# A list scheduler with other times for DMA landings and ScalarE handovers, and another table of ranks: the same instructions of an attention and two feed-forward layers in another order

## The chip, the cores and the metric

The kernel runs on one core of a Trainium2 chip. The time is the device time of one execution in microseconds. Of the kernel before, three runs gave 799.81, 796.45 and 795.07 us; their median is 796.45 us. The smallest change that a measurement of this kernel tells from none is about 0.5%, some 4 us.

## The reference: what is computed

Everything is float32. An attention of 2 batches x 8 heads, 768 positions of 64 elements, in which a query sees the keys of its own hash bucket alone, feeds two feed-forward layers over 1536 tokens:

```python
mask = q_bucket[:, :, :, None] == k_bucket[:, :, None, :]     # 6 sign bits of q @ proj, k @ proj
scores = np.where(mask, scale * np.matmul(q, k.transpose(0, 1, 3, 2)), -1000000000.0)
attn = np.exp(scores - np.max(scores, axis=-1, keepdims=True))
x = np.matmul(attn / (np.sum(attn, -1, keepdims=True) + 1e-09), v)      # -> 1536 x 512
h = np.maximum(x @ w_in, 0.0)                  # 512 -> 2048
x = (s * (h * h) + b) @ w_out                  # 2048 -> 512
out = (((x @ w1) * (x @ w2)) @ w3) @ w_out2    # 512 -> 1024 -> 1024 -> 512
```

## The kernel before, in words

**Numbers and products.** Each float32 operand is held as a high and a low part (fp32r), and each product is three matmuls. TensorE (PE) has the bulk: 4464 matmuls.

**Attention.** 16 heads of three units each, 48 units of 256 queries, numbered m = 0 to 47. A unit has two scores (`score0`, `score1`, tile `sc`, two PSUM buffers in all). For each: VectorE (DVE) takes the row maximum (`negm`, L499), a gate (L507) and a bias (L514); ScalarE (ACT) the exponential (`p`, L522). PE then turns p in three pairs (tile `t`, L536); each pair is split into high and low (`pt`) by ACT and DVE (L574, L578), the middle pair by ACT and GpSimd (POOL) (L557, L562, L568); PE multiplies by v (tile `o`, L542 and L543). ACT shifts half of `o` into `tmp` (L591), and DVE adds (`xf`, L595). The normalising factors are turned on PE too (tile `rt`, L632). The row masks `mm` come from `bits` (PE L463, DVE L468).

**First layer.** In batch 0's half (`h0`, `o0`) the weights arrive as raw float64 pieces of 512 KB (`raw_wi`, `raw_wo`), are converted in six steps (three on DVE, L322, L323 and L329; the others on ACT or POOL) into `w_wi`, `w_wo`, and are written back to memory (`kept_wi`, `kept_wo`). Batch 1's half (`h1`, `o1`) loads them again, 32 loads, into a pool of eight places (`wpool`), so a load waits on its queue until PE has read what stood in the place. PE makes `h`, then `x`, both at L717.

**Second layer.** When the last attention rows are done, the attention's tiles are closed and the second layer's opened (`reopen`). w3 and w_out2 are folded into one matrix on PE (tile `psw`, L929): 8 pieces of w_out2 and 16 of w3 are loaded raw and converted through two raw buffers (`raw2`). Then PE makes `a`, `b` (L717) and `y` (L968).

**What sets the order.** Every operation is recorded with its engine, an assumed time and a rank; a list scheduler (`Plan.emit`) then plays the program through on a clock of its own and issues on each engine, whenever it is free in that clock, the operation of the lowest cost: its rank, plus `LOSS` times the wait until it could start. Ranks come from due times, traced back from the end with the factors `SLACK` and the table `AT`, plus the table `SHIFT`. `TAIL` is what passes from an operation's end to its result, `LAG_TO` what the next engine needs, `PORT` names operations of DVE that can't run beside POOL's. Each engine's instructions then run on the chip in just the order that came out; DMAs are all issued by SyncE (SP), in one queue, in order.

Of the kernel before, what the change touches and what calls it, by code (L numbers as in the profile page):

```python
# [28 lines left out]
U = 256  # L29
# [5 lines left out]
LAG = 1  # L35
# [5 lines left out]
SLACK = dict(dma=0.3103, pe=0.4501, dve=0.4044, act=0.4169, pool=0.3583)  # L41
AT = {
# [10 lines left out]
}  # L53
HOLD = {"conv0_wi_0_0": 85.69, "conv0_wo_0_0": 118.54}
LATER = 1e9
SHIFT = {
# [24 lines left out]
    "kh_los/pool": 12.61, "kh_up0": -55.2, "kh_up1": -59.35, "kh_ups": -29.69, "kh_ups/dve": -53.6,  # L81
    "kh_ups/pool": 22.16, "lo00": 6.66, "lo01": -3.17, "lo0s": -50.9, "lo20": -30.38, "lo21": -5.15, "lo2s":
    -53.13, "load_b": 16.32, "load_p": -65.51, "load_qk0": -18.65, "load_qk1": 17.96, "load_qks": -36.78,
# [3 lines left out]
    "mks/dve": 16.57, "mks/pool": -23.64, "mq0": 33.96, "mq1": -43.58, "mqs": -30.74, "mqs/dve": 17.21,  # L87
# [5 lines left out]
    48.83, "qhs/pool": 83.58, "ql0": -40.32, "ql1": 8.23, "qls": 10.71, "qls/dve": -21.69, "qls/pool": -67.67,  # L93
# [15 lines left out]
}  # L109


def r32(ap):
    return ap.bitcast(F32)


class Slot:
# [17 lines left out]
class Plan:  # L134
# [42 lines left out]
    def locks(self, o, e):  # L177
        return e == "pool" or e == "dve" and o["key"].startswith(self.PORT)
# [4 lines left out]
    def emit(self):  # L183
        for o in reversed(self.ops):
            e, us, _ = o["ways"][0]
# [38 lines left out]
        t = 0.0  # L224
# [60 lines left out]
def lsh_attention_moe(ctx: ExitStack, tc: tile.TileContext, qT, kT, vl, projp, w_in, w_out, sv, bv, w12, w3T, wo2, out):  # L285
    nc = tc.nc
# [743 lines left out]
```

## Time and profile before

| | |
|---|---|
| median of three runs | 796.45 us |
| the profiled execution | 796.26 us, of which the span of its instructions is 794.5 us |
| PE busy | 760.0 us (96%) |
| DVE, ACT, POOL busy | 511.5, 393.6, 337.5 us |
| PE clock granted | full, but for the first microseconds |
| DMA | 110.83 MB in 36172 packets, mean 140 GB/s |

PE is busy through the whole span; the other engines are busy in its first two thirds, while attention, weight conversions and the first layer run, and nearly idle from 620 us on, where only `a`, `b` and `y` are left. The idle microseconds of PE and what ended them stand in the trace's waits; the same view for DVE shows where the engine that feeds it waited.

### The profile page before, as it was taken

To read this page: it belongs to the slowest core of one execution; us is meant where nothing else is said; L and a number is where in the kernel's file an instruction comes from. 1 tells how busy PE (TensorE), PEld (TensorE's weight loads), DVE (VectorE), ACT (ScalarE), POOL (GpSimd) and SP (SyncE) were. 2 spreads that over 40 slices of the span, in tenths; PEclk is the share of its full clock that TensorE was granted. 3 is DMA by queue.
4 is the path that set the end of the run, shared out by engine and by line. 5 is a ranking of instruction groups with operands and counts; after the bars stand their busy time and mean duration, and the time that the engine had idled before them with its cause. 6 is when DMAs were issued, how large, how long until landed. Compare 5 with 4: busy or idle time off the path is not lost.

```text
span 794.5 us, 12256 instructions
## 1 busy us (share of the span) xinstructions
PE 760.0 (96%) x4464; PEld 708.8 (89%) x4464; DVE 511.5 (64%) x1008; ACT 393.6 (50%) x754; POOL 337.5 (42%) x373
## 2 busy tenths in 40 slices
PE   5899999899999999999998999999999999999998
PEld 4788888789898998999998988989999999999996
DVE  4898898899899888899867666675687101010110
ACT  5788887886657546658543433433535111211112
POOL 3477668764755655545322232331327121121212
PEclk9999999999999999999999999999999999999999
DMA  8454344674657646573649886656231000000001
GB/s 211 108 134 119 91 104 116 204 210 134 196 175 233 176 160 184 174 219 108 212 159 324 280 293 242 223 178 207 83 105 54 1 1 14 26 14 21 7 14 66
DMA packets 36172, 110.83 MB, mean 140 GB/s; under 512 B 5136, under 2 KB 7312, under 8 KB 36112
## 3 DMA queue, kind: packets, MB, share of 16 engines
q1 hardware_dynamic: 36112, 110.06, 44.5%
q8 instruction: 35, 0.57, 0.3%
q14 instruction: 25, 0.20, 0.1%
HBM read 68.22 MB, written 24.12 MB: 116 GB/s over the span
## 4 chain that ended last, share of the span: by engine, by line
PE 62%; DVE 13%; ACT 9%; DMA 8%; issue 4%; POOL 4%; SPq 0%; ACTq 0%; POOLq 0%; DVEq 0%
PE h L717 10%; PE x L717 9%; PE a L717 8%; PE b L717 8%; PE y L968 8%; PE sc L489 4%; PE psw L929 4%; PE t L536 4%; ACT p L522 3%; DVE negm L499 3%; DMA raw_w<-in_w3T 3%; PE o L543 2%; PE o L542 2%; DVE pt L578 2%; ACT pt L574 1%
## 5 line engine op out<-in xcount | busy, mean ns | idle before, releaser
L717 PE MATMUL h<-x,w_wi 128*128 128x384 f32 x768 | 152.9, 341 | 2.3 <-DVE rl L793 0.9
L717 PE MATMUL x<-g,w_wo 128*128 128x384 f32 x768 | 151.5, 340 | 3.7 <-DMA w_wo<-kept_wo 1.4
L717 PEld LDWEIGHTS h<-x,w_wi 128*128 128x128 f32 x768 | 132.2, 188 | 8.4 <-DVE rl L793 3.3
L717 PEld LDWEIGHTS x<-g,w_wo 128*128 128x128 f32 x768 | 132.3, 188 | 8.2 <-issue 2.3
L522 ACT ACTIVATE p<-sc,bias,gate 128x768 f32<-128x768 f32 x96 | 95.6, 996 | 26.8 <-DVE bias L514 23.8
L953 DVE SCALAR_TENSOR_TENSOR ab<-b,ab 128x384 f32<-128x384 f32 x32 | 17.8, 557 | 132.4 <-ACT ab L950 102.4
L499 DVE TENSOR_REDUCE negm<-sc 128x1 f32<-128x768 f32 x96 | 90.9, 951 | 10.1 <-PE sc L489 9.6
L489 PE MATMUL sc<-k,q 128*128 128x384 f32 x384 | 89.9, 357 | 6.7 <-ACT p L522 5.2
L536 PE MATMUL t<-ident,p 128*128 128x128 f32 x576 | 85.8, 277 | 6.9 <-ACT p L522 4.3
L959 POOL TENSOR_TENSOR abt<-ab,abt 128x384 fp32r<-128x384 f32 x32 | 33.6, 1051 | 137.9 <-ACT abt L956 137.9
L536 PEld LDWEIGHTS t<-ident,p 128*128 128x128 f32 x576 | 68.0, 142 | 16.4 <-ACT p L522 7.4
L717 PE MATMUL a<-x,w_w 128*128 128x384 f32 x384 | 79.7, 335 | 0.0
L717 PE MATMUL b<-x,w_w 128*128 128x384 f32 x384 | 79.6, 335 | 0.0
L489 PEld LDWEIGHTS sc<-k,q 128*128 128x128 f32 x384 | 65.2, 193 | 11.6 <-ACT p L522 8.7
L542 PE MATMUL o<-pt,vv 128*128 128x256 f32 x288 | 74.1, 290 | 0.5 <-DVE gate L507 0.5
L543 PE MATMUL o<-pt,vv 128*128 128x256 f32 x288 | 72.3, 284 | 2.2 <-POOL pt L568 1.2
L578 DVE TENSOR_TENSOR pt<-t,pt 128x512 fp32r<-128x512 f32 x96 | 65.6, 685 | 9.8 <-ACT pt L574 9.0
L332 POOL TENSOR_TENSOR w_w<-raw_w,w_w 128x512 fp32r<-128x512 f32 x30 | 40.6, 1356 | 67.1 <-ACT w_w L330 66.6
L717 PEld LDWEIGHTS a<-x,w_w 128*128 128x128 f32 x384 | 67.8, 188 | 1.2 <-ACT ab L950 0.2
L956 ACT CAST abt<-ab 128x384 fp32r<-128x384 f32 x32 | 16.5, 516 | 104.7 <-PE y L968 96.7
L717 PEld LDWEIGHTS b<-x,w_w 128*128 128x128 f32 x384 | 67.9, 188 | 0.0
L968 PE MATMUL y<-whl,abt 128*128 128x512 f32 x288 | 67.5, 390 | 0.0
(99 smaller groups left out, 1283.3 us busy)
## 6 DMA issues: line engine op xcount, KB each, us to landing
kept_wo<-w_wo SPq DMA_DIRECT2D x24, 512.0 KB, 5.9
w_wo<-kept_wo SPq DMA_DIRECT2D x24, 512.0 KB, 5.2
raw_wi<-in_w_in SPq DMA_DIRECT2D x16, 512.0 KB, 4.5
raw_wo<-in_w_out SPq DMA_DIRECT2D x16, 512.0 KB, 4.6
kept_wi<-w_wi SPq DMA_DIRECT2D x16, 512.0 KB, 5.4
raw_w<-in_w SPq DMA_DIRECT2D x16, 512.0 KB, 4.4
w_wi<-kept_wi SPq DMA_DIRECT2D x16, 512.0 KB, 5.7
raw_w<-in_w3T SPq DMA_DIRECT2D x16, 512.0 KB, 4.4
```

What stands on the lines that cost most here:

```text
L332: lambda: nc.gpsimd.tensor_tensor(hl()[:, 1], w, r32(hl()[:, 0]), ALU.subtract),
L489: nc.tensor.matmul(sc()[:, i, :HALF], x[:, t], y[:, i * HALF : (i + 1) * HALF], start=st, stop=not st)
L499: lambda j=j, sc=sc: nc.vector.tensor_reduce(negm()[:, j : j + 1], sc()[:, :, :HALF], AX.XY, ALU.max, negate=True),
L522: lambda j=j, k=k, sc=sc: nc.scalar.activation(ps[j](), sc()[:, :, :HALF], AF.Exp, bias=bias()[:, j : j + 1], scale=gate()[:, j : j + 1], ...
L536: nc.tensor.transpose(tp()[:, e, j * P : (j + 1) * P], flat[:, c * P : (c + 1) * P], ident)
L542: nc.tensor.matmul(o()[:, :U], w, pt()[:, 0, e], start=(c == 0), stop=False)
L543: nc.tensor.matmul(o()[:, :U], w, pt()[:, 1, e], start=False, stop=(c == NC - 1))
L578: lambda tp=tp, pt=pt: nc.vector.tensor_tensor(pt()[:, 1], tp(), r32(pt()[:, 0]), ALU.subtract),
L717: nc.tensor.matmul(ps()[:, :n], x, y, start=(i == 0 and e == 0), stop=(i == len(terms) - 1 and e == 2))
L929: nc.tensor.matmul(ps(), w3()[:, p, c], wo()[:, q], start=(j == 0 and e == 0), stop=(j == 7 and e == 2))
L959: lambda: nc.gpsimd.tensor_tensor(abt()[:, 1], ab()[:, :TG], r32(abt()[:, 0]), ALU.subtract),
L968: nc.tensor.matmul(y(), abt()[:, p, c], wt()[:, q], start=(i == 0 and e == 0), stop=(i == DF2 // P - 1 and e == 2))
```

## The change

No instruction's work is changed. The scheduler's constants are: a DMA's result is given a further delay by its kind (`LATE`), handing over to ScalarE costs 0.085 in place of 0.037, several DVE and POOL operations are assumed to take longer (the bias 0.13 in place of 0.07), weight loads 1.3 in place of 1.46 (plus the new delay), and the tables `SLACK`, `AT`, `HOLD`, `SHIFT`, `AHEAD` and `LOSS` have other numbers throughout. Operations that may run on either of two engines can change sides: POOL has 15 instructions fewer and ACT 17 more.

```diff
-SLACK = dict(dma=0.3103, pe=0.4501, dve=0.4044, act=0.4169, pool=0.3583)
+SLACK = dict(dma=0.3391, pe=0.5535, dve=0.5716, act=0.4427, pool=0.4279)
 AT = {
-    "Wh": -4.86, "Wl": -0.88, "a": 53.23, "ab": 73.2, "abh": 79.81, "abl": 23.45, "add0": -0.46, "add1": -2.1,
+    "Wh": 6.26, "Wl": -2.82, "a": 32.88, "ab": 54.41, "abh": 54.36, "abl": 27.77, "add0": -2.95, "add1": 0.02,
...
-HOLD = {"conv0_wi_0_0": 85.69, "conv0_wo_0_0": 118.54}
+HOLD = {"conv0_wi_0_0": 67.61, "conv0_wo_0_0": 28.59}
...
-    LAG_TO = dict(dma=0.1, pe=0.055, dve=0.035, act=0.037, pool=0.085)
-    AHEAD, LOSS = dict(dma=0.079, pe=0.191, dve=0.043, act=0.334, pool=0.249), 21.169
+    LAG_TO = dict(dma=0.1, pe=0.055, dve=0.04, act=0.085, pool=0.095)
+    AHEAD, LOSS = dict(dma=1.714, pe=0.058, dve=0.072, act=0.268, pool=0.156), 39.709
...
+    LATE = dict(raw_=1.1, save_=1.5, again_w12=0.6, again_=0.3, load_=0.6, kh_=0.3, qh=0.3)
...
+    def late(self, o):
+        return next((v for k, v in self.LATE.items() if o["engine"] == "dma" and o["key"].startswith(k)), 0.0)
...
-                end = free[e] + self.TAIL[e]
+                end = free[e] + self.TAIL[e] + self.late(o)
...
-                    f"bias{j}{ph}", "dve", 0.07, LATER,
+                    f"bias{j}{ph}", "dve", 0.13, LATER,
...
-                f"shift{ph}", "act", 0.27, m + LAG + 0.9, lambda: nc.scalar.copy(tmp()[a], o()[z, :U]), [(o, 2)], [(tmp, 0)]
+                f"shift{ph}", "act", 0.39, m + LAG + 0.9, lambda: nc.scalar.copy(tmp()[a], o()[z, :U]), [(o, 2)], [(tmp, 0)]
...
-                f"raw_{key}", "dma", 1.46, LATER,
+                f"raw_{key}", "dma", 1.3, LATER,
...
-                f"square{b}", "dve", 0.47, rank + 0.01,
+                f"square{b}", "dve", 0.53, rank + 0.01,
```

**Place 1: DVE at the program's start.** In names, the first number after `sc_`, `negm_` or `gate_` is the unit, the last a running number; `sw` is a scale made of the scalar input `s_bc`, which a DMA brings. DVE before, from the second half of unit 0's mask on:

```order
L468 TENSOR_SCALAR mm_1_232<-bits_1_1_212,thr_72,sgn_73 128x384
L499 TENSOR_REDUCE negm_0_241<-sc_0_0_227 128x1
L499 TENSOR_REDUCE negm_0_241<-sc_0_1_236 128x1
L507 TENSOR_SCALAR gate_0_248<-negm_0_241 128x1 x2
L514 TENSOR_SCALAR bias_0_251<-negm_0_241,gate_0_248 128x1 x2
L499 TENSOR_REDUCE negm_1_274<-sc_1_0_261 128x1
L371 TENSOR_SCALAR sw_70<-s_bc_68 128x1
L507 TENSOR_SCALAR gate_1_291<-negm_1_274 128x1
L514 TENSOR_SCALAR bias_1_293<-negm_1_274,gate_1_291 128x1
L578 TENSOR_TENSOR pt_0_2_283<-t_0_2_276,pt_0_2_283 128x512
```

DVE now, in two pieces; from the scale on:

```order
L375 TENSOR_SCALAR sw_70<-s_bc_68 128x1
L428 CAST k1_0_185<-q1_0_181 64x768
L472 TENSOR_SCALAR mm_0_209<-bits_0_0_197,thr_72,sgn_73 128x384
L472 TENSOR_SCALAR mm_0_209<-bits_0_1_205,thr_72,sgn_73 128x384
L428 CAST k2_0_187<-mm_0_209 64x768
L472 TENSOR_SCALAR mm_1_230<-bits_1_1_218,thr_72,sgn_73 128x384
```

and from the first maximum of unit 0 on:

```order
L503 TENSOR_REDUCE negm_0_238<-sc_0_0_225 128x1
L503 TENSOR_REDUCE negm_0_238<-sc_0_1_232 128x1
L511 TENSOR_SCALAR gate_0_250<-negm_0_238 128x1
L472 TENSOR_SCALAR mm_1_230<-bits_1_0_242,thr_72,sgn_73 128x384
L518 TENSOR_SCALAR bias_0_253<-negm_0_238,gate_0_250 128x1
L511 TENSOR_SCALAR gate_0_250<-negm_0_238 128x1
L518 TENSOR_SCALAR bias_0_253<-negm_0_238,gate_0_250 128x1
L503 TENSOR_REDUCE negm_1_279<-sc_1_0_265 128x1
L511 TENSOR_SCALAR gate_1_288<-negm_1_279 128x1
L518 TENSOR_SCALAR bias_1_296<-negm_1_279,gate_1_288 128x1
```

The scale stood between the maximum and the gate of unit 1; now it stands ahead of the first masks, and its DMA is sixth on SP's queue, ahead of the weights, where it was the 18th. One half of head 1's mask (`mm_1`) now stands before unit 0's first bias.

**Place 2: ACT and DVE where unit 5 ends and unit 8 begins.** `p_8_0` is the exponential of unit 8's first score, `tmp_5` unit 5's shift, `xf_2` the sum that adds it. ACT before:

```order
L574 CAST pt_6_0_779<-t_6_0_743 128x512
L557 COPY pf_7_1_792<-t_7_1_781 128x512
L407 CAST q1_4_798<-t_4_423 128x768
L522 ACTIVATE p_8_0_821,ssum_2_666<-sc_8_0_756,bias_8_813,gate_8_795 128x768
L591 COPY tmp_5_838<-o_5_772 64x256
L522 ACTIVATE p_8_1_842,ssum_2_666<-sc_8_1_786,bias_8_813,gate_8_795 128x768
L574 CAST pt_6_2_855<-t_6_2_808 128x512
```

ACT now:

```order
L578 CAST pt_5_2_775<-t_5_2_743 128x512
L526 ACTIVATE p_7_1_780,ssum_2_670<-sc_7_1_730,bias_7_739,gate_7_737 128x768
L561 COPY pf_7_1_799<-t_7_1_792 128x512
L595 COPY tmp_5_815<-o_5_759 64x256
L526 ACTIVATE p_8_0_817,ssum_2_670<-sc_8_0_770,bias_8_813,gate_8_811 128x768
L411 CAST q1_4_834<-t_4_392 128x768
L578 CAST pt_7_0_849<-t_7_0_827 128x512
```

DVE before, round the sum that reads `tmp_5`:

```order
L514 TENSOR_SCALAR bias_8_813<-negm_8_777,gate_8_795 128x1
L499 TENSOR_REDUCE negm_8_777<-sc_8_1_786 128x1
L507 TENSOR_SCALAR gate_8_795<-negm_8_777 128x1
L514 TENSOR_SCALAR bias_8_813<-negm_8_777,gate_8_795 128x1
L595 TENSOR_TENSOR xf_2_551<-o_5_772,tmp_5_838 64x256
L636 TENSOR_TENSOR xf_2_551<-rt_5_818,xf_2_551 128x256
L499 TENSOR_REDUCE negm_9_864<-sc_9_0_844 128x1
```

DVE now:

```order
L503 TENSOR_REDUCE negm_8_797<-sc_8_0_770 128x1
L511 TENSOR_SCALAR gate_8_811<-negm_8_797 128x1
L518 TENSOR_SCALAR bias_8_813<-negm_8_797,gate_8_811 128x1
L599 TENSOR_TENSOR xf_2_566<-o_5_759,tmp_5_815 64x256
L503 TENSOR_REDUCE negm_8_797<-sc_8_1_806 128x1
L511 TENSOR_SCALAR gate_8_811<-negm_8_797 128x1
L518 TENSOR_SCALAR bias_8_813<-negm_8_797,gate_8_811 128x1
L503 TENSOR_REDUCE negm_9_856<-sc_9_0_842 128x1
```

The shift stood behind the exponential of `sc_8_0` and the sum behind both of unit 8's biases; now the shift stands ahead of that exponential, and the sum between the two maxima.

**Place 3: SP's queue where the second layer opens.** `raw_wo2` are the raw pieces of w_out2 (in the trace `raw_wo<-in_wo`; those of w3 are `raw_w<-in_w3T` there), `w_wo_1_0_0` to `w_wo_1_0_3` the four loads for batch 1's first `x` products. Before:

```order
L675 DMA raw_wo2_0_0_0_5504<-in_wo2 128x1024
L675 DMA raw_wo2_0_0_1_5523<-in_wo2 128x1024
L705 DMA w_wo_1_0_0_5552<-kept_wo_0_0_0_130 128x1024
L705 DMA w_wo_1_0_1_5569<-kept_wo_0_0_1_131 128x1024
L705 DMA w_wo_1_0_2_5582<-kept_wo_0_0_2_132 128x1024
L705 DMA w_wi_1_1_0_5602<-kept_wi_0_1_0_134 128x1024
L675 DMA raw_wo2_0_1_0_5647<-in_wo2 128x1024
L675 DMA raw_wo2_0_1_1_5664<-in_wo2 128x1024
L695 DMA kept_wo2_0_0_0_158<-w_wo2_0_0_0_5620 128x1024
L705 DMA w_wo_1_0_3_5698<-kept_wo_0_0_3_133 128x1024
```

Now:

```order
L709 DMA w_wo_1_0_0_5433<-kept_wo_0_0_0_130 128x1024
L709 DMA w_wo_1_0_1_5446<-kept_wo_0_0_1_131 128x1024
L709 DMA w_wo_1_0_2_5461<-kept_wo_0_0_2_132 128x1024
L709 DMA w_wo_1_0_3_5483<-kept_wo_0_0_3_133 128x1024
L679 DMA raw_wo2_0_0_0_5546<-in_wo2 128x1024
L679 DMA raw_wo2_0_0_1_5579<-in_wo2 128x1024
L679 DMA raw_wo2_0_1_0_5673<-in_wo2 128x1024
L709 DMA w_wi_1_1_0_5703<-kept_wi_0_1_0_134 128x1024
```

The fourth load stood behind four raw pieces, a load for batch 1's next weights and a store; now the four stand together ahead of every raw piece. Further on, all eight `raw_wo2` now stand ahead of the first `raw_w3`, where they alternated.

## Rows read from the trace of the kernel before

**Rows 1.** The page: busy us (share of the span) and instructions.
```profile
PE 760.0 (96%) x4464; PEld 708.8 (89%) x4464; DVE 511.5 (64%) x1008; ACT 393.6 (50%) x754; POOL 337.5 (42%) x373
```
**Rows 2.** Busy time by stretch: length, then busy us (instructions) of each engine.
```profile
0.00:20.00 20.00, 10.56 (x34) 8.57 (x35) 8.25 (x28) 10.01 (x15) 6.45 (x11) 0.92 0.82 210
20.00:180.00 160.00, 147.65 (x1026) 134.87 (x1025) 142.72 (x326) 131.55 (x262) 110.06 (x137) 1.00 0.52 137
180.00:420.00 240.00, 234.57 (x1474) 223.43 (x1473) 207.92 (x412) 145.61 (x283) 125.04 (x138) 1.00 0.56 177
420.00:600.00 180.00, 176.28 (x931) 163.46 (x930) 122.42 (x199) 67.16 (x118) 55.61 (x50) 1.00 0.61 211
600.00:794.00 194.00, 190.91 (x1007) 178.49 (x1005) 30.17 (x48) 39.32 (x79) 40.34 (x37) 1.00 0.06 22
```
**Rows 3.** Who waited for whom, 20 to 180 us: us in total, times, longest.
```profile
PE t L536 <- ACT p L522: 4.3, 8, 1.0
PE sc L489 <- ACT p L522: 2.7, 5, 0.8
...
DVE pt L578 <- ACT pt L574: 5.0, 13, 0.9
DVE xf L595 <- ACT tmp L591: 4.6, 13, 0.8
```
**Rows 4.** The chain that ended last, 10 to 25 us: start, us, what.
```profile
13.42 6.13 DMA s_bc<-in_sv
```
**Rows 5.** Timeline of DVE, 12 to 24 us: start, us, what [idle before].
```profile
14.59 0.33 DVE L514 TENSOR_SCALAR bias<-negm,gate 128x1 f32<-128x1 f32 x2
17.04 0.96 DVE L499 TENSOR_REDUCE negm<-sc 128x1 f32<-128x768 f32 x1 [2.12 <-PE sc L489]
19.57 0.15 DVE L371 TENSOR_SCALAR sw<-s_bc 128x1 f32<-128x1 f32 x1 [1.58 <-DMA s_bc<-in_sv]
...
22.01 0.67 DVE L468 TENSOR_SCALAR mm<-bits,thr,sgn 128x384 fp32r<-128x384 f32 x1
```
**Rows 6.** Timeline of all engines, 54 to 60 us.
```profile
56.51 0.21 DVE L514 TENSOR_SCALAR bias<-negm,gate 128x1 f32<-128x1 f32 x1
...
57.09 0.37 ACT L591 COPY tmp<-o 64x256 f32<-64x256 f32 x1 [0.33 <-PE o L543]
57.49 0.99 ACT L522 ACTIVATE p<-sc,bias,gate 128x768 f32<-128x768 f32 x1
57.49 0.43 DVE L595 TENSOR_TENSOR xf<-o,tmp 64x256 f32<-64x256 f32 x1 [0.77 <-ACT tmp L591]
...
58.62 0.97 PE L489 MATMUL sc<-k,q 128*128 128x384 f32 x4 [0.83 <-ACT p L522]
```
**Rows 7.** Timelines of SP and of PE, 416 to 434 us.
```profile
420.15 0.33 SPq L705 DMA_DIRECT2D w_wo<-kept_wo  x1
...
427.23 7.00 PE L717 MATMUL x<-g,w_wo 128*128 128x384 f32 x39 [1.38 <-DMA w_wo<-kept_wo]
```
**Rows 8.** The chain that ended last, 400 to 500 us.
```profile
by line: DMA raw_w<-in_w3T 20.7%; PE h L717 14.2%; PE psw L929 10.0%; DMA w_wo<-kept_wo 8.8%; PE x L717 7.5%; POOL w_w L332 6.6%; issue 5.8%; DVE rl L793 3.6%; DVE raw_w L329 3.5%; ACT raw_w L326 2.7%; ACT w_w L330 2.7%; DVE raw_w L322 2.3%
...
469.46 5.56 DMA raw_w<-in_w3T
...
478.87 1.33 POOL w_w L332
```
**Rows 9.** The same chain, 500 to 545 us.
```profile
501.41 2.08 PE h L717 x12
...
525.36 2.76 PE psw L929 x12
```
**Rows 10.** Timelines of SP: first piece of w_out2, last of w3.
```profile
401.62 0.81 SPq L675 DMA_DIRECT2D raw_wo<-in_wo  x2
...
530.26 0.33 SPq L675 DMA_DIRECT2D raw_w<-in_w3T  x1
```
**Rows 11.** DMA issues: count, KB each, median us to landing.
```profile
w_wo<-kept_wo SPq DMA_DIRECT2D x24, 512.0 KB, 5.2
...
raw_w<-in_w3T SPq DMA_DIRECT2D x16, 512.0 KB, 4.4
```
**Rows 12.** Groups of DVE by line: count, busy us, mean ns.
```profile
L329 DVE SCALAR_TENSOR_TENSOR raw_wi<-raw_wi 128x512 int32<-128x512 int32 x16 | 12.3, 771 | 0.2 <-ACT raw_wi L326 0.2
...
L322 DVE TENSOR_SCALAR raw_wi<-raw_wi 128x512 int32<-128x512 uint32 x16 | 8.1, 504 | 0.3 <-DMA raw_wi<-in_w_in 0.3
```

More of the change, by code (lines that the diff above doesn't have):

```diff
@@ L40 @@
 MORE = 1.0
-SLACK = dict(dma=0.3103, pe=0.4501, dve=0.4044, act=0.4169, pool=0.3583)
+SLACK = dict(dma=0.3391, pe=0.5535, dve=0.5716, act=0.4427, pool=0.4279)
 AT = {
[10 rows of a table removed]
[10 rows of a table added]
 }
-HOLD = {"conv0_wi_0_0": 85.69, "conv0_wo_0_0": 118.54}
+HOLD = {"conv0_wi_0_0": 67.61, "conv0_wo_0_0": 28.59}
 LATER = 1e9
 SHIFT = {
[24 rows of a table removed]
-    "kh_los/pool": 12.61, "kh_up0": -55.2, "kh_up1": -59.35, "kh_ups": -29.69, "kh_ups/dve": -53.6,
-    "kh_ups/pool": 22.16, "lo00": 6.66, "lo01": -3.17, "lo0s": -50.9, "lo20": -30.38, "lo21": -5.15, "lo2s":
-    -53.13, "load_b": 16.32, "load_p": -65.51, "load_qk0": -18.65, "load_qk1": 17.96, "load_qks": -36.78,
[3 rows of a table removed]
-    "mks/dve": 16.57, "mks/pool": -23.64, "mq0": 33.96, "mq1": -43.58, "mqs": -30.74, "mqs/dve": 17.21,
[5 rows of a table removed]
-    48.83, "qhs/pool": 83.58, "ql0": -40.32, "ql1": 8.23, "qls": 10.71, "qls/dve": -21.69, "qls/pool": -67.67,
[15 rows of a table removed]
[24 rows of a table added]
+    "kh_los": -59.71, "kh_los/dve": 12.37, "kh_los/pool": 5.83, "kh_up0": -107.46, "kh_up1": 17.49, "kh_ups":
[5 rows of a table added]
+    -147.6, "mks": 90.66, "mks/dve": -45.52, "mks/pool": -23.39, "mq0": 66.7, "mq1": -86.31, "mqs": -24.88,
[5 rows of a table added]
+    -20.53, "qhs/dve": 45.04, "qhs/pool": 139.08, "ql0": -65.54, "ql1": 26.19, "qls": 18.99, "qls/dve": 68.85,
[15 rows of a table added]
 }
@@ L436, in prep @@
             copy(f"split_h{ph}", (0.73, 0.8), q1, t, [(t, 0)], [(q1, 0)])
-            rest(f"split_l{ph}", 1.76, k2, t, q1, [(t, 0), (q1, 0)], [(k2, 0)])
+            rest(f"split_l{ph}", 1.8, k2, t, q1, [(t, 0), (q1, 0)], [(k2, 0)])
             mm = plan.tile(raw_p, 1, [P, S], F32R, "mm", f"mm_{n}")
@@ L566, in unit @@
                     plan.op(
-                        f"plo{c2}{ph}", "pool", 1.22, LATER,
+                        f"plo{c2}{ph}", "pool", 1.25, LATER,
                         lambda pf=pf, pt=pt: nc.gpsimd.tensor_tensor(pt()[:, 1], pf(), r32(pt()[:, 0]), ALU.subtract),
@@ L610, in norm @@
             plan.op(
-                f"ssum{b}", "dve", 0.07, at_,
+                f"ssum{b}", "dve", 0.09, at_,
                 lambda: nc.vector.tensor_scalar_add(ssum()[:, :, c], ssum()[:, :, c], 1e-9), mine, [(ssum, ("e", u))],
-                (("pool", 0.12, lambda: nc.gpsimd.tensor_scalar_add(ssum()[:, :, c], ssum()[:, :, c], 1e-9)),),
+                (("pool", 0.18, lambda: nc.gpsimd.tensor_scalar_add(ssum()[:, :, c], ssum()[:, :, c], 1e-9)),),
             )
@@ L682, in piece @@
                     ("dve", 0.34, ()), ("dve", 0.6, ()), ("act", 0.57, ("pool", 0.6)), ("dve", 0.6, ()),
-                    ("act", 0.57, ("pool", 0.6)), ("pool", 1.25, ("dve", 0.6)),
+                    ("act", 0.57, ("pool", 0.6)), ("pool", 1.29, ("dve", 0.61)),
                 )[k]
@@ L694, in piece @@
                 plan.op(
-                    f"save_{key}", "dma", 1.46, rank, lambda: nc.sync.dma_start(kept[keep], r32(hl()).rearrange("p a n -> p (a n)")),
+                    f"save_{key}", "dma", 1.3, rank, lambda: nc.sync.dma_start(kept[keep], r32(hl()).rearrange("p a n -> p (a n)")),
                     [(hl, 0), (hl, 1)], [("kept", keep)],
@@ L703, in again @@
             plan.op(
-                f"again_{key}", "dma", 1.46, LATER,
+                f"again_{key}", "dma", 1.3, LATER,
                 lambda: nc.sync.dma_start(r32(hl()).rearrange("p a n -> p (a n)"), kept[keep]), [("kept", keep)], [(hl, 0), (hl, 1)],
@@ L796, in relu2 @@
             plan.op(
-                f"gh{b}", "act", 0.46, rank + 0.01,
+                f"gh{b}", "act", 0.52, rank + 0.01,
                 lambda: nc.scalar.activation(gt()[:, 0], rl()[:, :TG], AF.Identity, bias=b_bc), [(rl, "q"), ("b", 0)], [(gt, 0)],
@@ L800, in relu2 @@
             plan.op(
-                f"gl{b}", "dve", 0.47, rank + 0.01,
+                f"gl{b}", "dve", 0.53, rank + 0.01,
                 lambda: nc.vector.scalar_tensor_tensor(
```

114 rows, old and new, of tables (AT, SHIFT) are left out of this document.

## The prediction

> **What bounds the kernel now.** I read the page first. PE is busy 760.0 of 794.5 us [rows 1], and no matmul is added or removed. An order can therefore win only where PE stands idle, and it loses wherever it makes PE stand idle somewhere else. The busy time by stretch says where that is [rows 2]: idle are 9.4 us of the first 20, 12.4 us from 20 to 180, 5.4 us from 180 to 420, 3.7 us from 420 to 600, and 3.1 us after that, where only `a`, `b`, `y` run. That is 34 us in all, and the start cannot all go, since the first matmul needs the first DMA. In the stretch from 20 to 180 DVE is the partner that is nearly full: 142.7 of 160 us.
>
> The waits of that stretch name the cause [rows 3]. PE waited 4.3 us to turn, and 2.7 us to score again, both for an exponential. DVE waited 4.6 us for ACT's shift `tmp` and 5.0 us for ACT's high parts `pt`. Later the picture is another: between 400 and 500 us the chain that ended last runs through the raw pieces of w3, their DMA (20.7%) and the conversions on POOL, DVE and ACT [rows 8]. PE covers that stretch with `h` and `x` of batch 1, so little idle time shows there, but the cover is thin.
>
> **The start.** The maximum of unit 1 began at 17.04 and took 0.96 us, so its gate could have run at 18.0. Ahead of the gate stood the scale `sw`, which waited 1.58 us for the scalar `s_bc` [rows 5], a DMA that landed 6.13 us after its issue [rows 4]. The new order issues that DMA sixth and puts the scale ahead of the first mask. So 1.58 us go. On the same chain one half mask is now done before unit 0's first bias, and that costs its 0.67 us [rows 5]. Together -0.9 us. Bounds: if the scale, now ahead of the first masks, holds them up for as long as it waits now, the 1.58 us are lost again and the half mask is paid for, +0.7. If the half mask is covered it is -1.6. I take -0.9.
>
> **The handovers inside attention.** From the row of the maximum (0.96), a gate and a bias (0.2 each) and the exponential (1.0) [rows 5, 6], a score needs about 2.5 us before PE may turn it or reuse its buffer, some 3 with one other operation in between. I counted PE work between the two in both orders, by the durations of its rows. Turns that stand less than 3.0 us of PE work behind their second score fall from 12 to 7 of 48; scores that stand less than 3.0 us behind the one whose buffer they take fall from 16 to 10 of 94. That is 40% fewer, and 40% of 7.0 us is 2.8 us.
>
> Unit 5 shows the other handover [rows 6]. DVE finished the bias at 56.72 and then stood 0.77 us for the shift, which ACT ran only at 57.09, behind an exponential and after a wait of 0.33 us for PE. The next exponential came behind the shift, at 57.49, and PE, which needed its buffer, stood 0.83 us at 58.62. In the new order the shift stands ahead of the exponential, and a sum stands between two maxima. Shifts directly behind an exponential fall from 13 to 6 of 48: 7 of 13 of the 4.6 us are 2.5 us. The two gains, 5.3 us, lie partly on the same chain, as unit 5 shows, so I take -4.0. Bounds: 0, if the waits only move to other instructions, and -11.6, if all of 4.3, 2.7 and 4.6 go.
>
> **Conversions brought forward.** Before unit 24's first maximum DVE now runs 11 conversion steps where it ran 6, and before unit 30's 26 where it ran 17. A step takes 0.50 to 0.77 us, say 0.68 [rows 12]: 3.4 and 6.1 us more of the engine that is nearly full. By the last unit nearly the same work has been done, and the earlier weights let `h` start 7 us of PE work earlier, which fills PE while DVE holds attention up. I take 0. Bounds: 0 and +6.1.
>
> **The load that came late.** PE stood 1.38 us for `w_wo` at 427.23; that load was issued at 420.15 [rows 7], so about 7 us passed, against a median of 5.2 [rows 11]. In the order before, only 33 matmuls of 0.173 us [rows 9], 5.7 us, lie between the last read of the tile in its place and its own first read. Now 117 instructions lie between, 19 us by their rows, and no load of batch 1 has under 15. The wait goes: -1.4, bounds 0 and -1.6.
>
> **The pieces of the second layer.** Here the change costs. A piece of w3 issued at 469.46 was done on POOL at 480.2 [rows 8], 10.7 us later; with two raw buffers that is 5.35 us a piece. Eight pieces of w_out2 and sixteen of w3 pass through. In the order before, 660 matmuls of the first layer (0.173) and 178 of the fold (0.230) [rows 9], 155 us, stand between the last turn of attention and the first use of the last w3 piece; now it is 543 and 179, 135 us. Needed are 23 x 5.35 + 10.7 = 134 us, so the pieces come just in time if they keep that pace. In the trace they did not: the first was issued at 401.62 and the last at 530.26 [rows 10], 128.6 us later, and 139 with the conversion, though at the end nobody pressed. Bounds are therefore 0 and +5; I take +1.0, nearer the pace of the piece itself.
>
> A rule bears on that pace. The median landing of such a piece is 4.4 us, and 5.2 for `w_wo` [rows 11]. The Trainium skill, "DMA: Bandwidth & Descriptors", section "Anatomy of one DMA", gives 2.0 us and the bytes at 436 GB/s for a copy of another issuing path, an estimate of 3.2 us for 512 KB; by that the pieces would need some 15 us less and the +1.0 would fall away, for a sum of -6.3. The trace does not agree with it, so the term stays.
>
> **The sum.** -0.9 - 4.0 + 0 - 1.4 + 1.0 = -5.3 us on the profiled execution's 796.26 us (span 794.5 and 1.8 around it) gives 791.0. That execution lies 0.2 us under the median of the runs, so it is used as it is. The end of the program cannot change: the last `y` products and two stores close it in both orders.
>
> **Rivals.** First, the fold waits: the pieces keep the trace's pace and not the piece's own, PE stands 4 us more than in my sum, and the time is 795, no change. For it: the chain of 400 to 500 us lies on these pieces already. Against it: w_out2's eight pieces are now issued without alternation, so w3's come in an unbroken row, and PE can do `h` and `x` meanwhile only if they stand ahead of the fold, of which fewer do now. I give it 0.22.
>
> Second, slower: DVE paces the stretch from 20 to 180 us, and nine more conversion steps ahead of unit 30 push its maxima back 6.1 us. From 180 to 420 PE is idle only 5.4 us, so it can't win this back. If DVE's own 17.3 us of idle time there don't shrink, the handovers give nothing, and the time is 796.3 + 6.1 - 0.9 - 1.4 + 1.0 = 801. It decides as soon as less than about 4 us of DVE's idle time goes. Against it: half of that idle is `tmp` and `pt`, on which the order did change. I give it 0.17.
>
> Third, the change doesn't do what it says: the waits for exponentials and shifts move to other pairs and only the load's 1.4 us goes, 796.3 - 0.9 - 1.4 + 1.0 = 795. I give it 0.11.
>
> **The chances.** My own case, 787 to 793, has 0.50. It lies partly within 0.5% of the time before, about what a measurement can tell from no change, so faster than 792.5 gets 0.50 with a little from better cases, within it 0.33 (the first and third rival), slower than 800.4 gets 0.17. The range that should hold the time 8 times in 10 goes from 785.0, where handovers give twice my term, to 799.0, where the second rival holds in part; my own case alone is 787 to 793.
>
> **What would show it.** Right: `sw` runs ahead of the first mask without a long wait, DVE's wait for `tmp` from 20 to 180 us is under 3 us, PE's waits for exponentials there are under 5, and no wait for `w_wo` stands near 420 us. For the pieces: if PE waits over 3 us for POOL's `w_w` in the fold, the first rival has come in. For DVE: if unit 30's maximum comes later than before by more than the PE work moved ahead of it, the second has. The forecast is wrong if PE's idle time from 20 to 420 us does not fall below 15 us (17.8 before), or if the idle time from 420 to 600 rises over 6 us.

## The result, and the profile after

The changed kernel takes 790.98 us (median of 9 runs, 789.54 to 792.85), the kernel before 797.12 (9 runs on the same chips). The ratio is 0.9915, with a 95% interval of 0.9891 to 0.9939: 6.8 us, between 4.9 and 8.7. Run again later beside other kernels, it came to 0.9920 (0.9900 to 0.9939). The forecast was 791.0. The profiled execution took 791.12 us, its span 789.0, 5.5 us less than before's.

The page's first line and the busy time by stretch, columns as in [rows 2]; here and below, a line number of after is that of before plus 4:

```profile
PE 756.0 (96%) x4464; PEld 712.3 (90%) x4464; DVE 509.1 (65%) x1008; ACT 404.3 (51%) x769; POOL 333.4 (42%) x358
```
```profile
0.00:20.00 20.00, 10.48 (x33) 8.80 (x34) 8.83 (x28) 9.72 (x14) 5.98 (x11) 0.95 0.76 211
20.00:180.00 160.00, 148.08 (x1021) 136.18 (x1020) 148.18 (x323) 130.03 (x258) 112.38 (x136) 1.00 0.54 143
180.00:300.00 120.00, 119.18 (x767) 115.32 (x767) 108.15 (x224) 79.87 (x154) 70.64 (x75) 1.00 0.62 184
300.00:420.00 120.00, 117.79 (x751) 114.33 (x749) 99.59 (x195) 73.51 (x144) 53.68 (x58) 1.00 0.52 166
420.00:600.00 180.00, 176.55 (x934) 165.83 (x933) 120.36 (x203) 76.11 (x131) 56.63 (x47) 0.99 0.61 211
```

The kernel before, for the two stretches that [rows 2] holds in one:

```profile
180.00:300.00 120.00, 116.21 (x731) 109.39 (x730) 104.63 (x205) 71.14 (x137) 71.41 (x76) 1.00 0.56 175
300.00:420.00 120.00, 118.36 (x745) 114.04 (x745) 103.30 (x208) 74.47 (x146) 53.63 (x62) 1.00 0.57 179
```

Count the matmuls. Up to 180 us after has done 1054, before 1060. From 180 to 300 it does 767 against 731, so it is 30 ahead at 300 us and 39 at 600. PE's busy time hides this, since a busy PE is not PE at its peak, so I took the time that PE lost from the starts of all matmuls: the distance from each to the next, less the distance at which its kind runs back to back (0.1735 us for `h`, `x`, `a`, `b`, `sc`, `bits`, 0.2275 for `psw`, `y`, 0.118 for `o`, 0.1085 for `t`, 0.028 for the last of a group of `t`).

| PE time lost, us | before | after | after, run again |
|---|---|---|---|
| ahead of the first matmul | 6.0 | 6.2 | 6.2 |
| from there to 40 | 13.8 | 12.5 | 11.9 |
| 40 to 180 | 24.6 | 25.0 | 24.8 |
| 180 to 300 | 12.3 | 7.1 | 8.0 |
| 300 to 420 | 7.4 | 7.8 | 7.7 |
| 420 to 600 | 8.9 | 8.4 | 8.5 |
| 600 to the last matmul | 1.4 | 1.1 | 1.0 |
| behind its start | 4.0 | 5.5 | 5.5 |

The rows add up to 4.8 us less in after, of the 5.5 by which the span fell. The gain was to come from 20 to 180 us; in these profiles 1.3 to 1.9 us of it came ahead of 40 us, nothing from 40 to 180, and 4.3 to 5.2 from 180 to 300. (e1 below shows that the start is worth more than this one profile of before tells.)

The waits of PE and of DVE from 20 to 180 us, against [rows 3]. First those of PE for DVE before, which [rows 3] leaves out:

```profile
PE o L543 <- DVE pt L578: 1.0, 2, 0.6
PE o L542 <- DVE gate L507: 0.5, 1, 0.5
...
PE bits L463 <- DVE pt L578: 0.2, 1, 0.2
```

After, PE and then DVE:

```profile
PE o L546 <- DVE xf L599: 2.1, 3, 1.1
PE t L540 <- ACT p L526: 2.0, 3, 1.3
PE t L540 <- DVE mm L472: 1.6, 2, 0.9
PE o L546 <- DVE gate L511: 1.5, 1, 1.5
PE t L540 <- DVE pt L582: 1.4, 4, 0.5
PE bits L467 <- DVE pt L582: 1.2, 1, 1.2
...
PE rt L636 <- DVE gate L511: 0.4, 1, 0.4
...
PE sc L493 <- ACT p L526: 0.3, 1, 0.3
PE t L540 <- DVE bias L518: 0.2, 1, 0.2
```
```profile
DVE pt L582 <- ACT pt L578: 2.5, 7, 0.8
DVE xf L599 <- ACT tmp L595: 2.4, 6, 0.6
```

What was announced happened: the waits for exponentials fell from 7.0 to 2.3 us, those of DVE for ACT from 9.6 to 4.9. But PE now waits 8.4 us for DVE (the rows of `xf`, `mm`, `gate`, `pt` and `bias` added up), where it was 1.7; all of PE's waits in this view add up to 11.7 us before and 11.6 after. One of these places, DVE at 98 us:

```profile
98.16 0.86 DVE L327 SCALAR_TENSOR_TENSOR raw_wi<-raw_wi 128x512 int32<-128x512 int32 x1
98.94 0.20 DVE L518 TENSOR_SCALAR bias<-negm,gate 128x1 f32<-128x1 f32 x1
99.07 0.94 DVE L503 TENSOR_REDUCE negm<-sc 128x1 f32<-128x768 f32 x1
99.93 0.41 DVE L599 TENSOR_TENSOR xf<-o,tmp 64x256 f32<-64x256 f32 x1
...
100.39 0.38 PE L546 MATMUL o<-pt,vv 128*128 128x256 f32 x1 [1.45 <-DVE gate L511]
```

The sum `xf` had its shift at 98.20; a conversion step, a bias and a maximum stand ahead of it. Until it has read `o`, the next unit can't write there: 1.45 us of PE. (The row names the gate, which ended last before PE went on; the buffer was the sum's.)

The load of `w_wo` no longer makes PE wait, but another wait stands 6 us behind its place. DVE and PE at 430 us, and the granted clock (third column from the end) behind it:

```profile
432.53 0.43 DVE L326 TENSOR_SCALAR raw_wo<-raw_wo 128x512 int32<-128x512 uint32 x1 [2.28 <-DMA raw_wo<-in_wo]
432.87 0.55 DVE L815 COPY acc<-x 128x384 f32<-128x384 f32 x1
...
433.47 0.79 PE L721 MATMUL h<-x,w_wi 128*128 128x384 f32 x3 [1.74 <-DVE acc L815]
```
```profile
433.00:434.00 1.00, 0.53 (x3) 0.53 (x4) 1.00 (x2) 0.00 (x0) 0.00 (x0) 1.00 0.94 320
434.00:435.00 1.00, 1.00 (x6) 1.00 (x5) 0.21 (x2) 0.68 (x1) 0.00 (x0) 0.64 1.00 365
435.00:436.00 1.00, 1.00 (x5) 1.00 (x4) 0.50 (x1) 0.46 (x1) 0.00 (x0) 0.50 0.80 311
```

DVE stood for a raw piece of w_out2 that landed 6.9 us after its issue (the median of these pieces is 5.6), and with it the sum behind it, on whose buffer PE depended. After this wait PE ran at half clock, 1.2 of 2.4 GHz, for some 3 us. And at the end of the program, ACT:

```profile
783.32 0.59 ACT L987 COPY yo<-y 128x512 f32<-128x512 f32 x1 [10.41 <-PE y L972]
785.53 0.59 ACT L987 COPY yo<-y 128x512 f32<-128x512 f32 x1 [1.62 <-DMA out<-yo]
```

The last three outputs now come 0.7 us apart and share two buffers, so the last copy waits 1.62 us for a store.

### The profile page after: what moved, and what is told of

Its sections match the earlier page's. It is cut to its first block, busy times and chain, and to the rows that moved or that the text cites. A ratio compares the mean times of both kernels' runs of the same rounds, so it can differ in the third digit from the quotient of the medians.

```text
span 789.0 us, 12252 instructions
## 1 busy us (share of the span) xinstructions
PE 756.0 (96%) x4464; PEld 712.3 (90%) x4464; DVE 509.1 (65%) x1008; ACT 404.3 (51%) x769; POOL 333.4 (42%) x358
## 4 chain that ended last, share of the span: by engine, by line
PE 70%; DVE 13%; DMA 5%; ACT 5%; issue 3%; POOL 2%; SPq 0%; ACTq 0%; POOLq 0%; DVEq 0%
PE x L721 14%; PE h L721 11%; PE b L721 8%; PE a L721 8%; PE y L972 8%; PE sc L493 5%; PE t L540 5%; DVE negm L503 3%; PE psw L933 3%; PE o L546 3%; PE o L547 3%; DVE pt L582 2%; DMA raw_wo<-in_wo 2%; ACT p L526 2%; DMA raw_w<-in_w3T 2%
## 5 line engine op out<-in xcount | busy, mean ns | idle before, releaser
L526 ACT ACTIVATE p<-sc,bias,gate 128x768 f32<-128x768 f32 x96 | 95.7, 997 | 30.0 <-DVE bias L518 16.5
L493 PE MATMUL sc<-k,q 128*128 128x384 f32 x384 | 87.5, 351 | 3.3 <-ACT p L526 2.4
L721 PE MATMUL a<-x,w_w 128*128 128x384 f32 x384 | 71.1, 334 | 0.0
L721 PE MATMUL b<-x,w_w 128*128 128x384 f32 x384 | 69.7, 335 | 0.0
L960 ACT CAST abt<-ab 128x384 fp32r<-128x384 f32 x32 | 16.5, 515 | 99.2 <-PE y L972 96.9
L572 POOL TENSOR_TENSOR pt<-pf,pt 128x512 fp32r<-128x512 f32 x48 | 64.9, 1352 | 5.6 <-ACT pt L568 2.4
```

What stands on the lines that cost most here:

```text
L493: nc.tensor.matmul(sc()[:, i, :HALF], x[:, t], y[:, i * HALF : (i + 1) * HALF], start=st, stop=not st)
L526: lambda j=j, k=k, sc=sc: nc.scalar.activation(ps[j](), sc()[:, :, :HALF], AF.Exp, bias=bias()[:, j : j + 1], scale=gate()[:, j : j + 1], ...
L572: lambda pf=pf, pt=pt: nc.gpsimd.tensor_tensor(pt()[:, 1], pf(), r32(pt()[:, 0]), ALU.subtract),
L721: nc.tensor.matmul(ps()[:, :n], x, y, start=(i == 0 and e == 0), stop=(i == len(terms) - 1 and e == 2))
```

## The experiments

All orders were written out as a list of the planner's operations and played through in place of the planner. Ratios are to before on the same chip, with 95% intervals.

**e1 to e4: one order up to a point, the other from there.**

```diff
 e1: before's list up to unit 6's second maximum,  then what is left of after's
 e2: after's list  up to unit 24's second maximum, then what is left of before's
 e3: after's list  up to unit 39's second maximum, then what is left of before's
 e4: before's to unit 24, after's to unit 39, then before's
```


> The order of before up to the second maximum of unit 6 (about 44 us), from there the order of after; at that point the two orders have done the same operations but for one each. If the start's term of -0.9 us holds, this is 0.9 us slower than after, 791.9. If, as the two traces suggest (18.6 us of PE time lost before unit 3 in both), the start gave nothing, it is 791.0, and a repeated profile shows unit 6's maximum at 43 to 44.5 us.

> The order of after up to the second maximum of unit 24 (about 143 us), then that of before. Theory 1, the gain is made by the order of units 24 to 39 itself: 796. Theory 2, the waits saved in units 6 to 24 were spent on conversions done ahead (3 us of DVE, 3 us of PE work, 26 operations), and the lead pays later: 792 or less. Theory 3, the handovers of units 6 to 24 gave their 4 us there: 793.

> The order of after up to the second maximum of unit 39 (about 285 us), then that of before. Under all theories that place the gain in attention: as after or better, since the last output copy no longer waits 1.6 us for a store; by the PE time lost in each part, 51.6 us up to there with after and 10.7 + 4.0 us behind it with before, against 10.1 + 5.5: 790. If the gain sat in the first layer of batch 1 or in the fold: 796.

> The order of before up to the second maximum of unit 24, that of after from there to the second maximum of unit 39, and before's again. Theory 1 (the order of units 24 to 39 itself): 791 to 792. Theory 2 (the lead of 3 us of DVE work at unit 24): 796 or more, since the lead has to be caught up with in the middle of attention. Theory 3: 796.

e1: 0.9976 (0.9960 to 0.9992); e2: 1.0144 (1.0118 to 1.0171); e3: 0.9945 (0.9921 to 0.9968); e4: 1.0151 (1.0121 to 1.0182). No theory had e2 and e4, and e3 lies between its two figures. The seam of e2 and e4 at unit 24 cost most: from 140 to 180 us PE lost 19.6 and 17.1 us, against 6.6 in before and 6.8 in after, and both ran at clock 0.50 for 7 us in it (e2 from 149 us, e4 from 152, during one wait of 7.4 us for DVE). Outside the seams, from 180 to 300 us, e2 with before's order lost 14.1 us although it had after's lead, e4 with after's order 8.9 without it. That favours theory 1, but behind a loss of 10 to 13 us at the seam it does not show it. In e3 the seam took some 4 us (280 to 300 us), and the time is still 4.4 us under before: most of the gain is made ahead of unit 39.

e1 met neither of its figures. By the ratios it is 4.5 us slower than after (0.9976 beside 0.9920; 2 to 6.5 us by the two intervals), and unit 6's maximum came at 47.0 us. What after does behind unit 6 is worth 1.9 us by e1's own ratio (0.6 to 3.2). Its seam shows no cost: from 40 to 180 us PE lost 25.1 us, as in after, and from 180 to 300 us 8.8, so that gain was kept. It was the start that was dear, with 16.3 us lost ahead of 40 us in place of 12.5 and 11.9:

```profile
21.84 0.15 DVE L375 TENSOR_SCALAR sw<-s_bc 128x1 f32<-128x1 f32 x1 [3.39 <-DMA s_bc<-in_sv]
```
```profile
22.96 0.69 PE L467 MATMUL bits<-q,pj_h 128*128 128x384 f32 x1 [2.55 <-DVE pt L582]
```
```profile
23.00:24.00 1.00, 1.00 (x3) 1.00 (x4) 1.00 (x2) 0.42 (x2) 0.00 (x0) 0.50 0.62 194
```

The scale waited not 1.58 us as in [rows 5] but 3.39; the same start waited 3.35 us in e4 and 2.77 in e8. SP issued the scalar's load at 16.1 us in all three, and at 13.42 in the profile that the prediction rested on. PE lost 16.5 us ahead of 40 us in e4 and in e8 too, and unit 3's maximum began at 30.4 to 30.8 us in the three, where it was 27.7 in that profile. So that profile of before caught a cheap start. How often a start is cheap is not known: in e10, whose queue differs by one more load ahead, the scale waited only 0.69 us and PE lost 13.2.

**e7 and e9: the scale alone, moved in before and put back in after.**

```diff
 e7, order of before: SP, DVE                 e9, order of after: SP, DVE
+s_bc<-in_sv   (7th DMA, 5th operation)      -s_bc<-in_sv   (6th DMA)
-s_bc<-in_sv   (18th operation)              +s_bc<-in_sv   (ahead of b_bc)
+sw<-s_bc      (ahead of the first mask)     -sw<-s_bc      (ahead of the first mask)
-sw<-s_bc      (ahead of unit 1's gate)      +sw<-s_bc      (ahead of unit 1's gate)
```


> The order of before with the load of the scalar fifth on SP's queue and the scale ahead of the first mask; nothing else. By the start's term of the prediction without the half mask: 1.58 us less. If the wait at the start is made good by later ones before unit 3's maximum, which began at 27.7 us in before and in after alike: no change, and that maximum stays within 0.3 us of 27.7.

> The order of after, with the scalar's load and the scale put back late as in before (the load ahead of the second scalar's, the scale ahead of unit 1's gate); nothing else. If the start is worth the 0.9 us of the prediction, or less: 791 to 792. If the wait of the scale is mostly longer than the 1.58 us of the first profile (2.8 to 3.4 us stood in three later profiles with the start of before), 793 to 795, and a wait of about 3 us stands before the scale.

e7: 0.9978 (0.9957 to 0.9999), 1.8 us faster than before, 0.1 to 3.4. e9: 0.9940 (0.9916 to 0.9964), beside 0.9920 for after on the same chip; the 1.6 us between them are within their intervals. Its profile shows a wait of 2.47 us and 16.3 us lost ahead of 40 us, but that execution took 798.1 us, 5.5 above e9's median. Both ratios are of one sign and fit 1 to 2 us; that the start's gain is made good before unit 3 is not borne out.

In after the scale waits too, ahead of the first masks:

```profile
7.48 0.15 DVE L375 TENSOR_SCALAR sw<-s_bc 128x1 f32<-128x1 f32 x1 [4.16 <-DMA s_bc<-in_sv]
```

Here the wait is nearly free. DVE stood 4.42 us at the same place in before, for ACT's `q`, and the first mask began at 8.80 us, before at 8.64.

**e5, e8, e11, e6: single operations moved, where a wait was read in the trace.**

```diff
 e5, order of after, DVE (six places between 98 and 172 us; one of them)
-L327 raw_wi<-raw_wi
 L518 bias<-negm,gate
+L599 xf<-o,tmp
 L503 negm<-sc
-L599 xf<-o,tmp
 L511 gate, L518 bias
+L327 raw_wi<-raw_wi
 e8, order of before (six places between 193 and 295 us; one of them), ACT
-L330 w_wo<-raw_wo
 L788 rl<-h x2
+L330 w_wo<-raw_wo
 e11, order of after, ACT, and: half mask behind the biases, two y products earlier
+L526 p<-sc (unit 1, second)
 L578 pt<-t x2
-L526 p<-sc (unit 1, second)
 e6, order of after, DVE, and: last y products in before's order
+L815 acc<-x
 L326 raw_wo<-raw_wo
-L815 acc<-x
```


> The order of after, with six conversion steps of the weights on DVE (at 98, 111, 117, 151, 154 and 172 us) moved behind the sum, low part or mask that stood behind them and that PE waited for, and two of those sums moved ahead of a maximum; nothing else. Theory A: between 20 and 180 us the handovers to ACT did get shorter, and the gain was spent because the conversions brought forward stand ahead of what PE waits for; then the waits of PE at 100.4 (1.7), 113.1 (1.4), 118.7 (0.6), 153.3 (1.0), 155.6 (0.9) and 173.5 us (0.7) shrink, and the time falls by 2 to 4.5 us, to 787 to 789. Rival B, DVE is full in that stretch and paces it: the same work is only late elsewhere, 790 to 792.

e5: 0.9965 (0.9945 to 0.9985), 2.8 us faster than before and so 4 slower than after; neither theory. The wait at 100 us went and others came. (The ACT step that follows the first of the six moved with it, behind an exponential.) Here ACT and PE at 114 us:

```profile
114.44 0.65 ACT L334 CAST w_wi<-raw_wi 128x512 fp32r<-128x512 f32 x1 [2.35 <-DVE raw_wi L333]
115.00 0.98 ACT L526 ACTIVATE p<-sc,bias,gate 128x768 f32<-128x768 f32 x1
...
116.13 0.97 PE L493 MATMUL sc<-k,q 128*128 128x384 f32 x4 [1.32 <-ACT p L526]
```

ACT's own conversion step stood 2.35 us for the step that I had moved back on DVE, with an exponential behind it, and PE waited for that exponential. A conversion passes through three engines in order; to move one step is to move a wait.

> The order of before with six local edits between 193 and 295 us, four on DVE (a square, two low parts ahead of a maximum, a conversion step behind a low part) and two on ACT (a conversion step behind two relu, a high part behind a copy): each puts first what PE waited for. If the 5.2 us that after loses less from 180 to 300 us come from where single operations stand, and not from DVE's load, PE's waits there (4.5 us over 0.3 us) go and the time falls by 3 to 4.5 us. If PE's next wait takes their place, under 1.5 us.

e8: 0.9992 (0.9975 to 1.0010), no difference. Of the six waits the largest stayed, 1.2 us for `rl`: its relu now stood ahead of ACT's conversion step but the square behind a DVE step that took 2.32 us (below). The expectation of 3 to 4.5 us has fallen, the theory is not settled by it, since only some of the waits went (3.4 us over 0.3 us were left of 4.5).

> The order of after with three edits: the half mask behind unit 0's biases (0.67 us), unit 1's second exponential ahead of two high parts on ACT, which it waited behind while PE stood 1.5 us, and two of the last y products two products earlier, so that the last copy finds its buffer free (1.6 us). If all three are on the path, 3 us faster than after: 788. If the first two are made good before unit 3, as the start's gain seemed to be, 789.5.

e11: 0.9929 (0.9905 to 0.9952), no better than after. The wait at 23 us shrank, and PE's next took its place; ahead of 40 us PE lost 12.8 us, no less than in after:

```profile
22.36 0.55 PE L540 MATMUL t<-ident,p 128*128 128x128 f32 x3 [0.77 <-ACT p L526]
...
25.55 0.66 PE L540 MATMUL t<-ident,p 128*128 128x128 f32 x4 [1.33 <-ACT pf L561]
```

In this profile PE also ran at half clock from 156.5 to 163.4 us, where no edit stands, and lost 10.0 us from 140 to 180, where after lost 6.8. Part of e11's time may lie there; the profile does not tell it apart.

> The order of after with two edits behind 430 us: one sum (acc) stands ahead of the first conversion step of a raw w_out2 piece, for whose DMA DVE stood 2.3 us with that sum behind it, and the last y products come in the order of before, so that the last copy of an output doesn't wait for the store that holds its buffer. If both waits are on the path, -1.7 and -1.6: 787.7, and PE's wait at 431 us is gone. If the first only moves to the next use of the late piece, 789.4.

e6: 0.9902 (0.9880 to 0.9925), not separable from after. The span behind the start of the last matmul fell from 5.5 to 4.0 us (in e11 to 4.1), as expected; against it PE waited 1.0 us at 766 us for an output copy, where after did not.

**e10: the conversions ahead, in before's order.**

```diff
 order of before; steps of conversions on DVE ahead of the first maximum of unit
-15: 0   18: 2   21: 4   24: 6    27: 9    30: 17
+15: 4   18: 7   21: 9   24: 11   27: 15   30: 26
```


> The order of before, with the conversions of the first weights, their loads and stores moved ahead to the units of attention where after has them, up to unit 30 (26 conversion steps on DVE ahead of unit 30 in place of 17); everything else as before. By the prediction's second rival DVE paces the stretch and this costs up to 6.1 us: 800 to 804. By the prediction's own term it costs nothing: 797 to 798. If the lead by itself were what made after faster from 180 us on, it would win some 4 us: 793 to 794.

e10: 1.0273 (1.0245 to 1.0301), 21.8 us slower, far over every price. Its first two stretches, and ACT and PE at 160 us:

```profile
20.00:180.00 160.00, 136.43 (x918) 122.45 (x917) 132.76 (x302) 121.19 (x239) 104.82 (x130) 0.98 0.49 129
180.00:300.00 120.00, 111.83 (x700) 104.36 (x700) 97.25 (x194) 71.55 (x141) 62.82 (x73) 0.99 0.54 157
```
```profile
159.77 0.65 ACT L330 ACTIVATE raw_wo<-raw_wo 128x512 f32<-128x512 f32 x1 [1.70 <-DVE raw_wo L327]
160.32 0.57 ACT L561 COPY pf<-t 128x512 f32<-128x512 f32 x1
...
161.04 0.42 PE L636 MATMUL rt<-ident,rb 128*128 128x128 f32 x2 [2.52 <-ACT pf L561]
```

DVE is busy 132.8 of 160 us and stands idle for 27, with fewer matmuls done (918, before 1026): it isn't full, so its load as such isn't what this costs. ACT waits 1.70 us for a conversion step with a copy of attention behind it, and PE 2.52 us for that copy; the clock is 0.50 from 162 to 164 us. This is one place of several: from 40 to 300 us PE lost some 20 us more than in before. After has as many of these steps ahead of unit 30 and pays nothing like it; why e10 does is shown at this place alone.

**e12: after, unchanged.**

> The kernel after, unchanged, beside the three others on the same chip, so that they can be compared with it: 0.9915 of before by its earlier runs, 0.989 to 0.994. Its second profile also shows which waits are the same in both and which vary from one execution to the next: the waits for the sum (4.7 us from 20 to 180 us) should stand, single waits for a DMA may not.

e12: 0.9920. The waits of the sum (2.1 and 1.5 us by the same rows) and of the masks (1.6) stand to a tenth; the one at 431 us, behind a DMA, fell: from 420 to 440 us PE lost 1.7 us, not 3.7.

## Why the prediction was right, and where it was not

The time was right to the tenth, which is luck. The term of -4.0 was not there from 40 to 180 us; 4.3 to 5.2 us that no term held came behind it, the start gave more than its term, and the end cost 1.5 us that the sum put at nothing. The sum also started from an execution 0.9 us under before's median of nine runs: the gain was 6.8 us, not 5.3.

- **The start**, -0.9: right in sign and too small. The scale alone gives 1.8 us (e7, 0.1 to 3.4), the whole order up to unit 6 some 4.5 (e1, 2 to 6.5), by its middle value the larger part of the gain. I took the wait from one execution, in which the load was issued 2.7 us earlier than in three later profiles and the clock did not fall a second time. Its half mask could not be told apart. "Without a long wait" did not come true (4.16 us), but that wait cost next to nothing.
- **The handovers**, -4.0: the step that failed is where the gain would be, and that it would be kept there. The waits for ACT fell by more than the 40% that I counted in the orders, yet from 40 to 180 us PE lost as much as before, since it now waited for DVE's sums, masks and low parts: for that stretch the third rival was right. A gain near the term in size, 4.3 to 5.2 us, stands at 180 to 300 us, where the prediction looked for none. Of the signs, the waits for exponentials and for `tmp` came in; PE's idle time from 20 to 420 us, which had to fall below 15 us, is 14.95 by the busy times of after's profile and 15.8 in e12.
- **The conversions**, 0: they cost DVE time where they stand. DVE was busy 5.5 us more from 20 to 180 us. Adding up how far each DVE operation exceeds the median of its kind (by over 0.12 us), 4.4 of these are operations that took longer: 0.3 us of excess in before, 4.7 in after. From 180 to 300 us it is the other way, 7.4 and 3.6. What they cost PE there is not shown apart from the handovers; e10 and e5 show only that neither order bears to have them moved alone.
- **The load**, -1.4, **and the pieces**, +1.0: the load's wait went. PE's waits for `w_w` from POOL in the fold rose from 0.3 to 0.9 us, and a piece that landed late cost 1.74 us and half the clock for 3 us at 431 in one profile of two. The stretch from 420 to 600 us lost 0.4 to 0.5 us less; the two terms give -0.4. The first rival did not come in.
- **The end**: "cannot change" was wrong. It is 1.5 us longer, because I looked at which operations close the program and not at the buffers that they share.
- **The second rival**, DVE as the pace: unit 30's maximum began at 195.0 us in place of 182.2, with 11.3 us more of PE work ahead of it, 1.5 us late; unit 39's was 6.8 us early with the same work done. By the letter of the sign this rival had come in, by 1.5 of its 6.1 us; it did not hold the kernel up, since the lead in work was kept. e10, far dearer with DVE idle for 27 of 160 us, suggests that such steps cost by where they stand and not by DVE's load.

Open is what makes the 4.3 to 5.2 us from 180 to 300 (3.5 in e1): the order of that stretch itself, the conversions done ahead, or DVE steps that no longer fall beside POOL's. The seams of e2 and e4 hide the answer, and no single edit moved it.

## What to carry to other kernels

A wait that goes shows the engine that is late next, so add up PE's waits by the engine waited for, before and after, not only the one that was aimed at. A step of a chain over three in-order engines isn't moved alone: ask what stands behind the next step on its engine. And the size of a wait for a DMA, with the place of the gain that hangs on it, needs more than one profile: here one cheap start hid most of what the start was worth.

## What the runs showed of the hardware

DVE's conversion steps, 0.5 to 0.8 us on the mean [rows 12], took up to 2.3 beside POOL. The kernel before at 235 us, POOL, DVE, ACT and PE:

```profile
235.13 1.84 POOL L414 TENSOR_TENSOR k<-t,q 128x768 fp32r<-128x768 f32 x1
235.22 2.31 DVE L329 SCALAR_TENSOR_TENSOR raw_wo<-raw_wo 128x512 int32<-128x512 int32 x1
...
237.56 0.66 ACT L330 CAST w_wo<-raw_wo 128x512 fp32r<-128x512 f32 x1 [2.79 <-DVE raw_wo L329]
238.12 0.86 ACT L788 ACTIVATE rl<-h 128x384 f32<-128x384 f32 x2
...
239.31 0.66 PE L536 MATMUL t<-ident,p 128*128 128x128 f32 x4 [1.24 <-DVE rl L793]
```

DVE began 0.09 us behind POOL, and its 2.31 us are the 1.75 that POOL still had and 0.56. ACT waited for it with two relu behind, and PE for them. The Trainium skill, "SBUF — State Buffer", section "Who interferes with whom", states that a DVE instruction with two inputs in SBUF contends with a GpSimd instruction that reads there, and that one blocks the other; this row agrees.

PE's clock fell after some of its long waits and not after others. Behind 1.74 us at 431 us it was 0.64 and then 0.50, behind 2.55 us at 23 us (e1) 0.50 for 3 us, behind 2.52 us at 161 us (e10) 0.50 for 2 us. It stayed at 1.00 behind 1.38 us at 427 us in before, 1.87 us at 161 us in e8 and even 2.60 us at 186 us in e10:

```profile
186.09 0.44 PE L467 MATMUL bits<-q,pj_h 128*128 128x384 f32 x1 [2.60 <-DVE pt L582]
```
```profile
187.00:188.00 1.00, 1.00 (x8) 0.69 (x6) 1.00 (x3) 0.00 (x0) 0.80 (x2) 1.00 1.06 397
```

In e11 it fell to 0.50 at 156 us behind waits of 0.87 and 0.69 us. After has the same two waits at 153 and 156 us and kept 1.00. So the length of the last wait alone does not tell whether the clock falls, and one profile does not either.
